# Loading K and V tiles through GpSimd's descriptor queue instead of SyncE's, in a decode kernel that streams 549 MB

## The chip, the cores and the metric

The kernel runs on one core of one Trainium2 chip. The metric is device time in microseconds (us). The kernel before took 1284.43 us as the median of 3 runs (1284.39 to 1284.6). Runs of one kernel agree within about 0.15%.

The names are those of the profile. PE is TensorE (matmuls), DVE is VectorE, ACT is ScalarE, POOL is GpSimd, SP is SyncE; SPq, POOLq and ACTq are loads that SyncE, GpSimd and ScalarE issue. A load goes from the large memory (HBM; the kernel before's page counts 549.03 MB read from it) to the core's own memory (SBUF) and is carried out by 16 DMA engines, as packets (12,975 of them on that page). The profile calls the queue of GpSimd's loads software_dynamic (q0) and those of SyncE and ScalarE hardware_dynamic (q1 and q10); "software queue" and "hardware queue" below mean these. A semaphore is a counter on which an engine can wait, here for a load to land (in the kernel before PE waits 3.2 us for wq) or for another engine's work (SyncE waits 18.0 us for PE's q projection).

## The reference

One decode step: an attention block over a long KV cache, mixed by a scalar gate with a gated MLP.

```
q      = x @ wq                                  # x: 1x448, wq: 448 x (16 heads x 256)
scores = (q . k_cache) / 16                      # 8 KV heads x 65536 keys x 256, bf16
a      = softmax(scores) @ v_cache  -> @ wo      # two query heads share a KV head
b      = ((gate * (gate > 0)) * up) @ W_down     # gate = x @ W_gate, up = x @ W_up, F = 1792
out    = g * a + (1 - g) * b                     # g = sigmoid(sum(x * gate_w))
```

K and V are 268 MB each and every byte is used once; everything else together is about 12 MB.

## The kernel before

K and V are cut into 32 tiles each, 128 partitions x 64 KB (8.4 MB) to a tile. Three such tiles fill the ring in SBUF. A tile of K is transposed in place on DVE and multiplied with q on PE (called QK); a tile of V is multiplied with the probabilities. "Gate/up" are W_gate and W_up together, four loads. The weights share a ring buffer: `wq`, then gate/up and `W_down`, live in buffer 2 before it becomes the home of K tile 2. Below, K0, K1, ... are tiles of K, V0, V1, ... tiles of V.

```python
# the order of the loads; each buffer is handed on round robin
order = [("wq", 0, 8.7), ("k", 0, TILE), ("gu", 0, 7.7), ("wd", 0, 3.8)]
for n in range(1, NT):
    order.append(("k", n, TILE))
    if n >= NTH - 1:
        order.append(("v", n - (NTH - 1), TILE))
# ... the last V tile in pieces, and wo ...

slot, held, freed = {}, {2: ["gu", "dn"]}, {}    # buffer 2 is free once gate/up and W_down were used on PE
r = 0
for kind, i, _ in order:
    if kind in ("k", "v") or (kind, i) in (("wo", 0), ("vp", 0)):
        slot[kind, i], freed[kind, i] = r, held.get(r, [])
        held[r] = [(kind, i)]
        r = (r + 1) % NRING
```

So K0 and K1 wait for nothing (buffers 0 and 1 start empty), K2 waits for `gu` and `dn` (the matmuls of gate/up and of W_down), and each later load waits for the matmuls that read its buffer last. Each engine runs its own list in order, and a wait holds up everything behind it in that list. In the kernel before SyncE waits 18.0 us for q in front of W_down, and K1, which itself waits for nothing, is issued behind W_down at 22.69 us. The lines of the program:

```python
# wq: two loads (rows of 24 KB, rows of 4 KB); q needs both
l_["wq"]  = dma("sp", t, "wq", ...)
l_["wqh"] = dma("sp", t + 0.01, "wqh", ...)
# W_down: goes where wq was, so it waits for the q projection
a3 = dma("sp", t, "wd", lambda e: e.dma_start(wd_sb, B_W_down...), [l_["q"]])
# a K tile
kd = dma("sp", t, "r%d" % sl, lambda e, n=n, sl=sl: e.dma_start(ring[sl][:], k_src(n)), free(("k", n)))
```

## Time and profile before

| | before |
|---|---|
| time, median | 1284.43 us |
| span of the profiled run | 1283.3 us |
| bytes loaded, mean rate | 549 MB, 428 GB/s |
| busy: DVE, PE, ACT, GpSimd | 49%, 33%, 5%, 0% |

Two parts of the kernel before's profile page: the share of DMA in 40 equal slices of the span (32 us each; tenths busy, and GB/s), and the queues (packets, MB, share of 16 engines' span).

```profile
DMA  9999999999999999999999999999999999999997
GB/s 398 431 436 432 432 437 432 432 434 432 436 427 436 434 434 429 432 436 434 429 432 437 434 434 432 436 427 432 435 438 425 432 440 434 430 427 440 431 408 313
...
q1 hardware_dynamic: 12930, 549.03, 99.2%
```

The stretches of the kernel before (us from the start; busy time and instruction counts of each engine; the last three columns are the granted PE clock, the DMA share and GB/s):

```profile
core 0: us, PE busy (x) PEld busy (x) DVE busy (x) ACT busy (x) POOL busy (x), PEclk, DMA share, GB/s
0.00:32.00 32.00, 11.17 (x72) 8.37 (x72) 8.31 (x35) 1.86 (x3) 4.09 (x21) 0.89 0.95 398
32.00:64.00 32.00, 19.98 (x232) 15.70 (x232) 18.64 (x12) 1.40 (x2) 0.00 (x0) 0.61 1.02 431
64.00:96.00 32.00, 10.56 (x96) 2.88 (x96) 30.22 (x15) 1.40 (x2) 0.00 (x0) 0.55 1.01 437
...
128.00:1240.00 1112.00, 356.50 (x3905) 126.46 (x3905) 550.24 (x343) 53.72 (x104) 0.00 (x0) 0.62 1.00 433
```

The DMA engines are never idle between the first microseconds and the tail: their share is 0.95 in the first 32 us and 1.00 to 1.02 in the stretches from there to 1240 us, and 433 GB/s were held for 1112 us. The kernel is bound by bytes over rate (549 MB at 433 GB/s make 1268 of the 1283.3 us); in this kernel a microsecond without transfers anywhere is a microsecond lost.

How long loads take, in the kernel before (what is loaded, who issues it, how many, KB, median us from issue to landing):

```profile
ring<-in_A_wq_dram SPq DMA_DIRECT2D x1, 512.0 KB, 11.0
ring<-in_A_k_cache_dram SPq DMA_DIRECT2D x32, 51.8
ring<-in_A_v_cache_dram SPq DMA_DIRECT2D x31, 36.7
...
ring<-in_B_W_up_dram SPq DMA_DIRECT2D x1, 224.0 KB, 35.4
```

A tile needs 19.4 us of all engines (8.39 MB at 433 GB/s). Landing 36.7 and 51.8 us after issue means that loads queue: when a tile is issued, most of another tile or more is still ahead of it. By estimate, 17 us of other transfers (36.7 less 19.4) or more are in front of a tile when it is issued, against 0.33 us for an issue on SyncE, so this queue can hide what an issue costs.

SyncE's timeline (start, duration, what, how many; the last line merges K1, K2 and K3):

```profile
22.32 0.33 SPq L441 DMA_DIRECT2D ring<-in_B_W_down_dram  x1
22.69 37.56 SPq L452 DMA_DIRECT2D ring<-in_A_k_cache_dram  x3
```

K1 was issued at 22.69 us, directly after W_down. The chain of work that ended last, of the same kernel (start, duration, what), at the place where K2 is released:

```profile
52.92 5.17 PE ST L347 x54
58.09 1.34 PE A_ps L358 x27
59.44 0.33 SPq L452
59.81 43.62 DMA ring<-in_A_k_cache_dram
```

PE finishes QK of K0 (L347), then the W_down product (L358), and at 59.44 us K2 is issued. K2's first packet starts at 60.9 us, and the last packet of K1 ends at 63.2 us in the packet records: K2 arrives at the engines just in time. The slack is small: where the engines are idle (experiment 2), the first packet follows SyncE's issue of K2 by 0.96 us, so K2 was ready at about 60.4 us here, by estimate 0.5 us before the first engine came free and 2.8 us before the last.

### The profile page before, as it was taken

To read this page: it belongs to the slowest core of one execution; us is meant where nothing else is said; L and a number is where in the kernel's file an instruction comes from. 1 tells how busy PE (TensorE), PEld (TensorE's weight loads), DVE (VectorE), ACT (ScalarE), POOL (GpSimd) and SP (SyncE) were. 2 spreads that over 40 slices of the span, in tenths; PEclk is the share of its full clock that TensorE was granted. 3 is DMA by queue.
4 is the path that set the end of the run, shared out by engine and by line. 5 is a ranking of instruction groups with operands and counts; after the bars stand their busy time and mean duration, and the time that the engine had idled before them with its cause. 6 is when DMAs were issued, how large, how long until landed. Compare 5 with 4: busy or idle time off the path is not lost.

```text
span 1283.3 us, 9919 instructions
## 1 busy us (share of the span) xinstructions
PE 427.0 (33%) x4600; PEld 162.9 (13%) x4600; DVE 633.6 (49%) x421; ACT 61.5 (5%) x116; POOL 4.1 (0%) x21
## 2 busy tenths in 40 slices
PE   3633332334123432224331243321433323233235
PEld 2401110111001210001110111100111101011111
DVE  2597633465533655434555444555434555335600
ACT  0000000000000000000000000000000000000000
POOL 1000000000000000000000000000000000000000
PEclk8656666656666565667665666655666656666567
DMA  9999999999999999999999999999999999999997
GB/s 398 431 436 432 432 437 432 432 434 432 436 427 436 434 434 429 432 436 434 429 432 437 434 434 432 436 427 432 435 438 425 432 440 434 430 427 440 431 408 313
DMA packets 12975, 549.67 MB, mean 428 GB/s; under 512 B 1283, under 2 KB 3590, under 8 KB 3974
## 3 DMA queue, kind: packets, MB, share of 16 engines
q1 hardware_dynamic: 12930, 549.03, 99.2%
q8 instruction: 36, 0.59, 0.2%
q14 instruction: 5, 0.04, 0.0%
q10 hardware_dynamic: 4, 0.00, 0.0%
HBM read 549.03 MB, written 0.00 MB: 428 GB/s over the span
## 4 chain that ended last, share of the span: by engine, by line
DVE 34%; DMA 32%; another core or an unknown queue 16%; PE 15%; SPq 1%; ACT 1%; issue 1%
DVE ring L335 30%; DMA ring<-in_A_k_cache_dram 27%; PE ST L347 7%; PE O L378 6%; DMA ring<-in_B_W_up_dram 3%; DMA ring<-in_A_wo_dram 2%; DVE P_sb L480 1%; SPq L521 1%; DVE nmb L458 1%; PE PT L485 1%; PE M_ps L429 1%; PE M_ps L432 0%; ACT ptp L494 0%; DVE o_sb L389 0%
## 5 line engine op out<-in xcount | busy, mean ns | idle before, releaser
L335 DVE STREAM_TRANSPOSE ring<-ring 128x2048 uint32<-128x2048 uint32 x256 | 565.4, 2275 | 410.0 <-DMA ring<-in_A_k_cache_dram 410.0
L347 PE MATMUL ST<-ring,xm 128*16 128x512 bf16 x2048 | 224.2, 612 | 755.2 <-DVE ring L335 755.2
L347 PEld LDWEIGHTS ST<-ring,xm 128*16 128x16 bf16 x2048 | 61.9, 120 | 903.0 <-DVE ring L335 794.6
L378 PE MATMUL O<-ring,ptp 128*4 128x512 bf16 x2048 | 149.0, 453 | 34.3 <-DMA ring<-in_A_v_cache_dram 30.3
L460 ACT ACTIVATE P_sb<-ST,nmb 128x512 bf16<-128x512 f32 x32 | 45.3, 1414 | 1112.7 <-DVE nmb L458 1112.7
L458 DVE TENSOR_REDUCE nmb<-ST 128x1 f32<-128x512 f32 x32 | 22.0, 689 | 110.7 <-PE ST L347 110.7
L378 PEld LDWEIGHTS O<-ring,ptp 128*4 128x4 bf16 x2048 | 54.5, 99 | 128.5 <-issue 58.3
L389 DVE CAST o_sb<-O 128x512 bf16<-128x512 f32 x8 | 5.5, 692 | 80.5 <-PE O L378 80.5
L480 DVE TENSOR_TENSOR P_sb<-P_sb,hs 128x1024 bf16<-128x1024 bf16 x16 | 18.9, 1222 | 8.7 <-ACT hs L474 8.7
L485 PE MATMUL PT<-identb,P_sb 128*128 128x128 bf16 x128 | 16.6, 310 | 15.5 <-DVE P_sb L480 14.7
L429 PE MATMUL M_ps<-xT,ring 128*128 128x1 bf16 x84 | 9.4, 205 | 16.3 <-DMA ring<-in_B_W_up_dram 16.3
L485 PEld LDWEIGHTS PT<-identb,P_sb 128*128 128x128 bf16 x128 | 12.3, 140 | 18.3 <-DVE P_sb L480 18.3
L494 ACT COPY ptp<-PT 128x256 bf16<-128x256 bf16 x32 | 10.3, 375 | 23.0 <-PE PT L485 23.0
L307 PE MATMUL M_ps<-ring,P_sb 128*128 128x256 bf16 x64 | 10.1, 335 | 3.2 <-DMA ring<-in_A_wq_dram 3.2
L429 PEld LDWEIGHTS M_ps<-xT,ring 128*128 128x128 bf16 x84 | 7.2, 151 | 16.9 <-issue 16.5
L460 ACT ACTIVATION_READ_ACCUMULATOR P_sb<-ST,nmb 128x1 f32 x32 | 8.5, 267 | 0.0
L307 PEld LDWEIGHTS M_ps<-ring,P_sb 128*128 128x128 bf16 x64 | 7.6, 120 | 5.5 <-issue 3.3
L432 PE MATMUL M_ps<-xT,ring 128*64 128x1 bf16 x56 | 7.8, 276 | 0.0
L412 DVE STREAM_TRANSPOSE ptp<-P_sb 128x128 uint32<-128x128 uint32 x1 | 0.3, 313 | 13.5 <-ACT P_sb L411 13.5
L470 PE MATMUL M_ps<-identf,hs 128*2 128x128 f32 x8 | 2.6, 321 | 10.0 <-DVE hs L468 10.0
L432 PEld LDWEIGHTS M_ps<-xT,ring 128*64 128x64 bf16 x56 | 5.4, 191 | 0.4
L358 PE MATMUL A_ps<-ring,attnT 128*1 128x224 bf16 x64 | 4.6, 305 | 2.5 <-DMA ring<-in_A_wo_dram 2.5
(72 smaller groups left out, 60.1 us busy)
## 6 DMA issues: line engine op xcount, KB each, us to landing
ring<-in_A_v_cache_dram SPq DMA_DIRECT2D x1, 4096.0 KB, 29.3
ring<-in_A_wq_dram SPq DMA_DIRECT2D x1, 3072.0 KB, 10.2
ring<-in_A_wo_dram SPq DMA_DIRECT2D x1, 2240.0 KB, 31.8
ring<-in_A_v_cache_dram SPq DMA_DIRECT2D x1, 2048.0 KB, 23.6
ring<-in_B_W_down_dram SPq DMA_DIRECT2D x1, 1568.0 KB, 20.6
ring<-in_B_W_gate_dram SPq DMA_DIRECT2D x1, 1344.0 KB, 32.6
ring<-in_B_W_up_dram SPq DMA_DIRECT2D x1, 1344.0 KB, 35.3
ring<-in_A_v_cache_dram SPq DMA_DIRECT2D x1, 1024.0 KB, 25.6
```

Source lines behind the costliest of these rows:

```text
L307: ins = e.matmul(QN_ps, xw3[:, k_, 31 - j:159 - j], rhs, start=(j == 0 and kt == 0), stop=(j == J - 1 and kt == R3))
L335: return lambda e: e.transpose(v, v)
L347: ins = e.matmul(bank[32 * w:32 * w + 16, :], xm[:, x0:x0 + 16], ktv[sl][:, u0:u0 + 16, c, :, r_], start=(b == 0 and c == 0 and r_ == 0), ...
L378: ins = e.matmul(OP[h % 2][32 * g:32 * g + 4, :], ptp[h % 2][:, col:col + 13:4], ring[sl][:, k * 512:(k + 1) * 512], start=(a == 0 and k < ...
L429: e.matmul(GU_ps[:, c:c + 1], wf3[which][:, kt * F + ft:(kt + 1) * F:FT], xT[:, kt:kt + 1], start=(kt == 0), stop=False, skip_group_check= ...
L432: ins = e.matmul(GU_ps[64 * half:64 * half + 64, c:c + 1], wfh[which][:, ft:F // 2:FT], xT[:, R3 + half:R3 + half + 1], start=False, stop= ...
L458: smax[n] = op("dv", tk + 22, lambda e, n=n, NM=NM, t_=t_: e.tensor_reduce(NM[:, t_:t_ + 1], ST[n % 2][:], AX.X, ALU.max, negate=True), [q ...
L460: aexp[n] = op("ac", tk + 23, lambda e, n=n, t_=t_, NM=NM, RS=RS: e.activation(P_sb[:, t_:2048:4], ST[n % 2][:], ACTF.Exp, bias=NM[:, t_:t ...
L480: rsc = op("dv", tt, lambda e, X=X, pb=pb: e.tensor_tensor(pb, pb, X[:, 12:16].unsqueeze(1).to_broadcast([128, 256, 4]), ALU.mult), [h7, a ...
L485: ins = e.transpose(PT[rd][:, s * 128:(s + 1) * 128], P_sb[:, (rd * 8 + s) * 128:(rd * 8 + s + 1) * 128], identb[:, :])
L494: ins = e.copy(dst, src)
L521: dep = dma("sp", t, "vp%d" % i, lambda e, sl=sl, n=n, lo=lo, hi=hi: e.dma_start(ring[sl][:, lo * 256:hi * 256], v_src(n)[:, lo * 256:hi * ...
```

## The change

The stated change is to load K and V tiles through GpSimd's descriptor queue instead of SyncE's. The queue's kind changes (software_dynamic in the profile, not hardware_dynamic), and so does which list a load stands in. K0 stays on SyncE with a semaphore of its own, because this program counts a semaphore's landings in the order of one engine's list.

```diff
-                kd = dma("sp", t, "r%d" % sl, lambda e, n=n, sl=sl: e.dma_start(ring[sl][:], k_src(n)), free(("k", n)))
+                kd = dma("sp" if n == 0 else "gp", t, "rk0" if n == 0 else "r%d" % sl, lambda e, n=n, sl=sl: e.dma_start(ring[sl][:], k_src(n)), free(("k", n)))
 ...
-                    dep = dma("sp", t, "r%d" % sl, lambda e, sl=sl, n=n: e.dma_start(ring[sl][:], v_src(n)), free(("v", n)))
+                    dep = dma("gp", t, "r%d" % sl, lambda e, sl=sl, n=n: e.dma_start(ring[sl][:], v_src(n)), free(("v", n)))
```

The order of instructions on PE, DVE and ACT is the same in both kernels. On GpSimd, 62 loads follow the 17 small setup instructions. On SyncE, the weights, K0, wo and the pieces of the last V tile remain.

## The prediction

> **What bounds the kernel now.** The page's queue part has queue 1 at 99.2% of 16 engines' span; the slices hold 425 to 440 GB/s nearly throughout, and the stage table gives a DMA share of 1.00 and 433 GB/s from 128 to 1240 us. DVE (49%) and PE (33%) have slack. The packet records show the tiles as 64 KB packets, median 2.42 us each. So time is bytes over rate, plus about 2 us of start and 5 of tail.[...]
>
> **What the change does.** 62 tile loads (K tiles 1 to 31, V tiles 0 to 30) move from SyncE's instruction stream to GpSimd's; bytes, buffers and the orders on PE, DVE and ACT stay. Weights, K tile 0 and the last V tile (in pieces) stay on SyncE.
>
> *Steady state.* Loads are issued when their buffer comes free: K tiles a median 51.8 us before landing, V tiles 36.7, against 19.4 us of transfer each. So most of a tile is queued ahead[...].[...] Cost about 0, plus an unknown small rate difference.
>
> *Start: the real cost.* Before, K1 sits behind the W_down load in SyncE's stream, which waits for the q projection: issued at 22.7 us. After, K1 waits for nothing and leaves GpSimd at about 7 us (its last setup instruction ends at 6.0).[...] With 64 KB packets on one side and the remaining 24 KB and 4 KB wq packets on the other, nearly all of K1's 8 packets per engine pass before wq is complete: wq lands at about 30 us instead of 12, q ends at 40 (22.3), K0 lands at 49 (31.5), gate/up at 57 (39.1), W_down at 61. Then PE needs gate/up (13.5 us), QK of K0 (5.2) and W_down (1.3) before K2 may overwrite the weights' buffer: issued at about 77 us instead of 59.4. All issued so far has landed by about 61, and K3 stands behind K2. So the DMA engines idle for about 17 us that a DMA-bound kernel never gets back. Before, K2 was issued about 3 us before K1 ended.
>
> *End.* wo's 1792-byte packets now alternate with V29's and V30's 64 KB ones: V30 lands about 1 us later. Cost 0 to 2 us.
>
> **Prediction.** 1284.4 + 17 (start) + about 2 (end, issue latency, rate) = **1303 us**, range 1287 to 1316. Faster by over 2%: 0.01; within: 0.74; slower: 0.25.
>
> **What would show it.** The stage table at 60 to 80 us nearly without DMA; wq and gate/up landing about 18 us later (L307's wait); K2's issue near 77 us; 433 GB/s after 128 us; short issues on GpSimd.
>
> **What would make it wrong.** If software descriptors are cut into small packets (4 KB), SyncE's loads win the round robin and the gap shrinks to about 4 us: time near 1290.[...]

The sum is 1284.4 + 17 (the start) + about 2 (the end, the latency of issues, the rate), which is 1303 us. At the marks, passages are cut that rested on no trace or run of this case but stood behind some of its terms and odds: a bound on the rate (behind the 0.01 for "faster by over 2%"), what hides the cost of an issue (behind "Cost about 0" and the latency of issues), how the engines serve two queues (behind the landings at the start, and so behind the 17 us), and two of the dangers (behind the 0.25 for "slower"). "The round robin" in the danger that remains is engines taking turns between two queues by packet; the trace of the changed kernel and experiment 8 show it, below.

## More of the kernel before

In SyncE's list K1 stands behind W_down, which waits for q. That order, not a dependency, keeps K1 away from the loads of the start.

## The result, and the profile after

| | before | after |
|---|---|---|
| time, median | 1284.51 us (4 runs: the 3 above and one more) | 1303.18 us (4 runs, 1302.92 to 1303.93) |
| span of the profiled run | 1283.3 us | 1301.1 us |
| ratio | | 1.0144, 95% interval 1.013 to 1.0159 |

Ratios here and below are the mean time of one kernel's runs over that of the other's runs of the same rounds, so not quite the ratio of the medians quoted. The 18.7 us are far outside the noise.

The same two parts of the changed kernel's page:

```profile
DMA  9859999999999999999999999999999999999997
GB/s 403 374 226 450 422 438 428 440 426 440 428 432 439 424 436 436 432 440 425 438 424 438 430 438 430 436 433 428 438 430 436 428 438 428 436 430 440 427 416 325
...
q0 software_dynamic: 8928, 520.10, 92.5%
q1 hardware_dynamic: 4002, 28.94, 5.4%
```

92.5% of the engines' time now belongs to the software queue. There is one hole, in the second and third slices (374 and 226 GB/s). The stretches of the changed kernel:

```profile
0.00:32.00 32.00, 1.12 (x9) 0.95 (x10) 5.94 (x24) 1.49 (x2) 4.78 (x22) 1.00 0.98 410
32.00:64.00 32.00, 15.12 (x120) 12.37 (x118) 14.93 (x16) 0.37 (x1) 0.00 (x0) 0.69 0.89 380
64.00:96.00 32.00, 18.56 (x215) 12.11 (x219) 23.30 (x14) 1.40 (x2) 1.06 (x2) 0.61 0.53 222
...
128.00:1240.00 1112.00, 352.52 (x3856) 124.34 (x3860) 563.66 (x353) 55.50 (x108) 30.08 (x57) 0.61 1.00 433
```

The last line is the important negative finding: over 1112 us the software queue moved data at 433 GB/s, the rate of the hardware queue to three digits. The packet records say the same: 7936 packets of 64 KB at a mean of 2425.2 ns, against 8064 at 2424.8 ns before. The loss lies in the stretches from 32 to 64 us (share 0.89 instead of 1.02) and from 64 to 96 us (0.53 instead of 1.01). In the packet records no packet of a kernel's load runs from 61.9 to 80.4 us: a gap of 18.5 us, against a difference of 18.7 us in time.

Loads of the changed kernel:

```profile
ring<-in_A_wq_dram SPq DMA_DIRECT2D x1, 512.0 KB, 30.5
ring<-in_A_k_cache_dram POOLq DMA_DIRECT2D x31, 51.9
ring<-in_A_v_cache_dram POOLq DMA_DIRECT2D x31, 36.7
...
ring<-in_B_W_up_dram SPq DMA_DIRECT2D x1, 224.0 KB, 54.8
...
ring<-in_A_k_cache_dram SPq DMA_DIRECT2D x1, 49.3
```

In the steady state K and V tiles take as long from issue to landing as before (51.9 and 36.7 us). The rest of the start is late by one tile: the small part of wq (512 KB, the rows of 4 KB) lands 30.5 us after issue instead of 11.0, the last part of gate/up 54.8 instead of 35.4 (19.4 us later, which is one tile's transfer).

GpSimd's timeline (start, duration, what, how many, and in brackets its idle time before and who ended it; the second line merges K2 and K3):

```profile
5.95 0.74 POOL L452 DMA_DIRECT2D ring<-in_A_k_cache_dram  x1
79.16 1.06 POOL L452 DMA_DIRECT2D ring<-in_A_k_cache_dram  x2 [72.46 <-PE A_ps L358]
```

K1 leaves at 5.95 us instead of 22.69, before the data that precedes it in the order of use. Then GpSimd waits 72 us for PE, and K2 goes out at 79.16 instead of 59.44. The chain that ended last, at the same place as before:

```profile
72.39 5.11 PE ST L347 x52
77.50 1.36 PE A_ps L358 x28
78.86 0.30 issue
79.16 0.53 POOL ring L452
79.69 42.09 DMA ring<-in_A_k_cache_dram
```

PE's work in front of K2 is as long as before (5.1 and 1.4 us); it is done 19.4 us later.

How K1 gets ahead can be counted in the packet records. Between 10 and 31 us, 120 packets of K1 (64 KB, 2.42 us each) and 121 packets of wq's small part (4 KB, 0.16 us each) started, and 17 packets of K0 on engines that were through with wq: about one for one. The records don't name the engine, but joined by their times into 16 sequences they alternate: while K1 is under way, the next packet is of the other queue in 190 of 215 cases (where two engines change at once, the joining can mix them up). So in this trace the engines took turns between the two queues by packet, and 125 of K1's 128 packets had started when wq's last one ended, at 31.2 us. In bytes, 64 KB against 4 KB is a split of 16 to 1 in favour of the queue with the larger packets.

### The profile page after: what moved, and what is told of

Read it like the earlier page. It is cut to its first block, busy times and chain, and to the rows that moved or that the text cites. A ratio compares the mean times of both kernels' runs of the same rounds, so it can differ in the third digit from the quotient of the medians. Undisturbed runs are those within 1.5% of the kernel's fastest.

```text
span 1301.1 us, 9919 instructions
## 1 busy us (share of the span) xinstructions
PE 424.5 (33%) x4600; PEld 161.7 (12%) x4600; DVE 633.5 (49%) x421; ACT 61.6 (5%) x116; POOL 37.0 (3%) x83
## 3 DMA queue, kind: packets, MB, share of 16 engines
q0 software_dynamic: 8928, 520.10, 92.5%
## 4 chain that ended last, share of the span: by engine, by line
DVE 33%; DMA 31%; another core or an unknown queue 17%; PE 16%; SPq 1%; ACT 1%; issue 1%; POOL 0%
DVE ring L335 30%; DMA ring<-in_A_k_cache_dram 27%; PE ST L347 6%; PE O L378 6%; DMA ring<-in_A_wq_dram 2%; DMA ring<-in_A_wo_dram 2%; DVE P_sb L480 1%; SPq L521 1%; DVE nmb L458 1%; PE M_ps L307 1%; PE PT L485 1%; PE M_ps L429 1%; PE M_ps L432 0%; ACT ptp L494 0%
## 5 line engine op out<-in xcount | busy, mean ns | idle before, releaser
L378 PE MATMUL O<-ring,ptp 128*4 128x512 bf16 x2048 | 146.2, 447 | 34.6 <-DMA ring<-in_A_v_cache_dram 30.6
L378 PEld LDWEIGHTS O<-ring,ptp 128*4 128x4 bf16 x2048 | 53.7, 97 | 127.1 <-issue 54.8
L517 POOL DMA_DIRECT2D ring<-in_A_v_cache_dram x31 | 16.4, 528 | 945.4 <-PE ST L347 941.7
L452 POOL DMA_DIRECT2D ring<-in_A_k_cache_dram x31 | 16.6, 535 | 248.6 <-PE O L378 151.4
L307 PE MATMUL M_ps<-ring,P_sb 128*128 128x256 bf16 x64 | 10.0, 335 | 22.3 <-DMA ring<-in_A_wq_dram 22.3
L429 PE MATMUL M_ps<-xT,ring 128*128 128x1 bf16 x84 | 9.5, 205 | 16.3 <-DMA ring<-in_B_W_up_dram 16.3
## 6 DMA issues: line engine op xcount, KB each, us to landing
ring<-in_A_v_cache_dram SPq DMA_DIRECT2D x1, 4096.0 KB, 30.5
```

The costliest lines, as they stand in the source:

```text
L307: ins = e.matmul(QN_ps, xw3[:, k_, 31 - j:159 - j], rhs, start=(j == 0 and kt == 0), stop=(j == J - 1 and kt == R3))
L378: ins = e.matmul(OP[h % 2][32 * g:32 * g + 4, :], ptp[h % 2][:, col:col + 13:4], ring[sl][:, k * 512:(k + 1) * 512], start=(a == 0 and k < ...
L429: e.matmul(GU_ps[:, c:c + 1], wf3[which][:, kt * F + ft:(kt + 1) * F:FT], xT[:, kt:kt + 1], start=(kt == 0), stop=False, skip_group_check= ...
L452: kd = dma("sp" if n == 0 else "gp", t, "rk0" if n == 0 else "r%d" % sl, lambda e, n=n, sl=sl: e.dma_start(ring[sl][:], k_src(n)), free((" ...
L517: dep = dma("gp", t, "r%d" % sl, lambda e, sl=sl, n=n: e.dma_start(ring[sl][:], v_src(n)), free(("v", n)))
```

## The experiments

Each was correct; "before" was timed beside them on the same chip (1285.0 to 1285.2 us as the median of 7 runs in each of the three groups). Theory A is the prediction's: one gap in front of K2, because K1 pushes gate/up a tile later. Rival B blames the software path itself, for each load. Rival C blames the delay of wq and the q projection, the most visible symptom at the start.

### 1. K1 back on SyncE, the other 61 tile loads on GpSimd

```diff
-kd = dma("sp" if n == 0 else "gp", t, "rk0" if n == 0 else "r%d" % sl, ...)
+kd = dma("sp" if n <= 1 else "gp", t, "rk%d" % n if n <= 1 else "r%d" % sl, ...)
```

> Only K tile 1 goes back to SyncE's stream (behind the W_down load, issued near 22.7 us); the other 61 tile loads stay on GpSimd. Theory A (the loss is one gap of the DMA engines in front of K tile 2, because K1's early packets push gate/up a tile later; the software queue itself costs nothing): 1284.5 us, within 2; gate/up wait of PE ends near 39 us, K2 issued near 60 us, DMA share at or above 0.99 from 64 to 96 us. Rival B (each software-issued load costs some 0.3 us of latency or rate, 62 of them make 18.7 us): 1302 to 1303. Rival C (K1 delays wq and with it the q projection): as A, 1284.5.

Measured: 1285.17 us, ratio 0.9999 (0.9982 to 1.0015). Its stretch from 64 to 96 us:

```profile
64.00:96.00 32.00, 8.80 (x80) 2.46 (x84) 28.13 (x14) 1.40 (x2) 0.53 (x1) 0.55 0.99 426
```

Moving one load of 62 takes back the whole loss. B falls: 61 software-issued loads cost nothing that can be measured (the interval leaves room for about 2 us). The end is that of the changed kernel (wo still shares the engines with V29 and V30), so the end costs nothing beyond that either.

### 2. The kernel before, with only K1 on GpSimd

```diff
-kd = dma("sp", t, "r%d" % sl, ...)
+kd = dma("gp" if n == 1 else "sp", t, "rk%d" % n if n <= 1 else "r%d" % sl, ...)
```

> The kernel before with only K tile 1 moved to GpSimd (issued near 6 us); 61 tile loads stay on SyncE. Theory A: 1303 us, within 2, with DMA share about 0.53 from 64 to 96 us and gate/up complete near 57 us. Rival B (a cost for each software load): 1284.8, one load costs 0.3. Rival C: as A.

Measured: 1303.61 us, ratio 1.0142 (1.0127 to 1.0157). Its stretch from 64 to 96 us:

```profile
64.00:96.00 32.00, 18.91 (x211) 11.69 (x209) 22.87 (x14) 1.41 (x2) 0.00 (x0) 0.61 0.54 226
```

The gap runs from 61.8 to 80.3 us. One load alone makes the whole loss; with experiment 1 it is both necessary and sufficient.

### 3. The kernel before, with only K1 on ScalarE's hardware queue

```diff
-kd = dma("sp", t, "r%d" % sl, ...)
+kd = dma("ac" if n == 1 else "sp", -7 if n == 1 else t, "rk%d" % n if n <= 1 else "r%d" % sl, ...)
```

> The kernel before with only K tile 1 moved to ScalarE's hardware queue, issued near 1.5 us; no software descriptors at all. Theory A: the queue's kind doesn't matter, only that K1 runs beside the loads of the start: gap of 17 to 19 us in front of K2, 1302 to 1305 us. Rival B (software descriptors): 1284.5 us, within 1.

Measured: 1302.95 us, ratio 1.0137 (1.0121 to 1.0152), with no software queue in the kernel (its page lists none; K1's 8.39 MB are in q10, hardware_dynamic). Its stretch from 64 to 96 us:

```profile
64.00:96.00 32.00, 18.55 (x211) 11.97 (x211) 23.28 (x14) 1.40 (x2) 0.00 (x0) 0.61 0.54 230
```

So the kind of queue does not matter here (1302.95 us with K1 on ScalarE's hardware queue, 1303.61 with K1 on GpSimd's software queue). What matters is that K1 runs in a queue beside SyncE's, early.

### 4. The changed kernel, with K1 waiting for the q projection

```diff
-..., free(("k", n)))
+..., free(("k", n)) + ([l_["q"]] if n == 1 else []))
```

> The changed kernel, but K1's load on GpSimd waits until the q projection is done, so wq is undisturbed and q ends near 22.3 us as before. Theory A (what counts is when gate/up lands, and K1's 19.4 us of packets still pass before it): gate/up complete near 57 to 58 us, K2 issued near 78 us, gap of 15 to 18 us, 1300 to 1303 us. Rival C (the delay of wq and q is the cause): K2 issued near 60 us, 1285 us, within 2.

Measured: 1303.43 us, ratio 1.0143 (1.0128 to 1.0158). K1 was issued at 22.22 us, half a microsecond earlier than in the kernel before, wq was undisturbed, and nothing was gained. K1 and K2 in GpSimd's timeline, then a load's landing and a wait of PE, from this run's loads and waits:

```profile
22.22 0.74 POOL L452 DMA_DIRECT2D ring<-in_A_k_cache_dram  x1 [16.22 <-PE M_ps L307]
79.27 1.06 POOL L452 DMA_DIRECT2D ring<-in_A_k_cache_dram  x2 [56.30 <-PE A_ps L358]
```

```profile
ring<-in_B_W_up_dram SPq DMA_DIRECT2D x1, 224.0 KB, 54.8
```

```profile
PE M_ps L429 <- DMA ring<-in_B_W_up_dram: 36.1, 1, 36.1
```

PE's wait for wq is 3.3 us (3.2 before, 22.3 in the changed kernel), and its wait for gate/up is 36.1 us instead of 16.3. Gate/up lands exactly as late as in the changed kernel, because K1's packets still pass before it; K2 is issued at 79.27 us. C falls. Compare with the kernel before: same issue time of K1, but there it stood behind gate/up in one queue, here it ran beside it in another. The issue time is not what counts; the order at the engines is.

### 5. The changed kernel, with K1 waiting until gate/up has landed

```diff
+                l_["a1"] = a1                       # the four loads of gate/up
 ...
-..., free(("k", n)))
+..., free(("k", n)) + (l_["a1"] if n == 1 else []))
```

> The changed kernel, all 62 tile loads on GpSimd, but K1's load waits until the gate/up weights have landed (near 39 us; W_down's 3.8 us of transfer covers the wait and the issue). Theory A: no gap, K2 issued near 60 us, DMA share at or above 0.98 from 64 to 96 us, 1284.5 to 1286.5 us. If something else of the software queue costs time (rate, latency, the end beside wo), that remainder shows here above 1286.5.

Measured: 1286.16 us, ratio 1.0008 (0.9993 to 1.0023): no gap, as predicted, and not to be told from before. Its stretch from 64 to 96 us:

```profile
64.00:96.00 32.00, 7.37 (x72) 2.05 (x76) 27.62 (x14) 1.39 (x2) 0.53 (x1) 0.55 0.99 429
```

All 62 loads can go through GpSimd at no cost that these runs can tell from noise (the interval leaves room for 3 us), if K1 is ordered behind gate/up by a semaphore that does what the single list did.

### 6. The changed kernel, with gate/up loaded before K0

```diff
-order = [("wq", 0, 8.7), ("k", 0, TILE), ("gu", 0, 7.7), ("wd", 0, 3.8)]
+order = [("wq", 0, 8.7), ("gu", 0, 7.7), ("k", 0, TILE), ("wd", 0, 3.8)]
```

> The changed kernel, K1 still issued near 6 us, but SyncE loads gate/up before K tile 0, so that PE can do gate/up and W_down before QK of K0. Theory A: wq still lands near 31 us, q ends near 42, gate/up has landed near 38, W_down lands near 62, K2 issued near 63 to 64 us: a gap of 2 to 4 us, 1286 to 1289 us. If K1's early issue cost something other than the late K2, 1300 or more.

Measured: 1290.46 us, ratio 1.0044 (1.0027 to 1.006), outside the expected 1286 to 1289. The direction is right (13 us of the loss are back), the size is not: the gap is 5.0 us (63.1 to 68.05). K2 was issued at 66.80 us, not at 63 to 64. W_down landed at 63.56 us instead of 62, and from there to the issue 3.2 us passed where the expectation left 1 to 2. The timeline shows most of that second part:

```profile
63.70 2.77 PE L358 MATMUL A_ps<-ring,hT 128*1 128x224 bf16 x28 [8.21 <-DMA ring<-in_B_W_down_dram]
```

The W_down product now follows W_down's landing directly. It took 2.77 us after 8.2 us of idle PE, against 1.51 us in the kernel before's timeline, directly behind other matmuls. (Whether the idle time before it made the product slower was not tested.)

### 7. The changed kernel, with only half of K1 issued early

```diff
+if n == 1:
+    kd  = dma("gp", t, "rk1a", ... ring[sl][:, 0:16384] ..., free(("k", n)))
+    kd2 = dma("gp", t, "rk1b", ... ring[sl][:, 16384:32768] ..., l_["a1"])   # after gate/up
 ...   # the last four of K1's eight transposes wait for kd2
```

> The changed kernel, but only half of K1 (4 MB) is issued near 6 us; the other half waits until gate/up has landed. Theory A: gate/up lands half a tile later (9.7 us, near 49 us), the gap is about half a tile less about 1 us of slack: 8 to 9.5 us, 1292 to 1295 us. A cost of any early concurrency that doesn't scale with its bytes (q late, one blocked queue): 1300 or more.

Measured: 1293.82 us, ratio 1.007 (1.0055 to 1.0085), with a gap of 8.85 us. The last part of gate/up:

```profile
ring<-in_B_W_up_dram SPq DMA_DIRECT2D x1, 224.0 KB, 45.2
```

That is 9.8 us later than before, half a tile. Half the bytes in front of gate/up make about half of the loss (8.8 of 18.7 us). The packets are halved too (128 of 32 KB), so their number in front of gate/up is that of the changed kernel: it is their bytes that count.

### 8. The changed kernel, with K1 as 16 loads of 4 KB rows

```diff
+for c in range(16 if n == 1 else 0):
+    kd = dma("gp", t, "rk1", ... ring[sl][:, c * 2048:(c + 1) * 2048] ..., free(("k", n)))
```

> The changed kernel, but K1 is loaded by 16 loads of 128 rows of 4 KB, all issued from GpSimd from about 6 us, instead of one of 128 rows of 64 KB: the same bytes, as early. Theory A with round robin by packet: each of SyncE's packets (4, 64, 10.7, 1.8 KB) now lets only one 4 KB packet of 0.16 us pass. From 7.5 us to the end of gate/up there are about 51 of SyncE's packets per engine, so gate/up lands about 8 us later than before (46 us), W_q's small half near 14 us, the gap is about 7 us, 1290 to 1293 us. If the engines share time or bytes evenly between the queues: gate/up again lands near 57 us, gap of 18 us, 1302 to 1304 us. If K1 only gets what SyncE leaves: no gap, 1285.

Measured: 1292.37 us, ratio 1.0054 (1.0037 to 1.0071), with a gap of 6.2 us (63.7 to 69.95). Gate/up:

```profile
ring<-in_B_W_up_dram SPq DMA_DIRECT2D x1, 224.0 KB, 43.4
```

That is 8.0 us later than before. The bytes and the time of the first issue (5.94 us) are those of the changed kernel; the size of a packet differs, and more than half of the loss is gone. (The 16 issues take 8.55 us together, 0.53 us for each 512 KB; the engines need about 1.2 us for as much at 433 GB/s, so the issuing did not hold K1 back.) By estimate, gate/up's 8.0 us of delay are about 50 of K1's packets per engine at 0.16 us each, against about 50 of SyncE's per engine from 7.5 us to the end of gate/up (a sixteenth of those in the packet records of the kernel before and of the changed one). So the engines take turns by packets here, neither by bytes nor by time: gate/up landed at 47.3 us, not near 57.

### The series

| kernel | gate/up lands later by (us) | gap (us) | longer than before by (us, medians) |
|---|---|---|---|
| before | 0 | none | 0 |
| K1 early in 4 KB packets (8) | 8.0 | 6.2 | 7.2 |
| half of K1 early (7) | 9.8 | 8.85 | 8.8 |
| changed kernel | 19.4 | 18.5 | 18.7 |
| K1 waits for q (4) | 19.4 | 18.65 | 18.2 |

The gap is the delay of gate/up less 0.8 to 1.8 us, which fits the slack of the kernel before.

No experiment pointed to a version that beats both kernels. The kernel before has no gap between its start and its tail to take back, and the software queue gives the same rate.

## Why the prediction was right

- *The bound.* Right. The DMA share from 128 to 1240 us was 1.00 before and after, at 433 GB/s in both.
- *Steady state free.* Right. K and V tiles land as long after issue as before, packets take the same 2.42 us, and experiment 1 (61 loads through GpSimd) is at 0.9999. GpSimd needs 0.53 us for an issue in the steady state against 0.33 us on SyncE. In the one place where an issue is exposed, at the end of the gap, 1.54 us pass from PE's last matmul to K2's first packet with GpSimd, and 0.98 us with SyncE (experiment 2). Elsewhere, by the estimate above, the 17 us of transfers in front of a tile can hide these 0.6 us, and experiment 1 shows no loss (0.9999).
- *K1 passes in front.* Right, and shown by the packet records (190 changes of queue in 215) and by experiment 8 (gate/up 8.0 us late instead of 19.4). The wording "wq lands at about 30 us" holds for its small part alone (31.7 us); the large part landed at 13.4 us. For q both are needed, so nothing hung on it.
- *The gap in front of K2.* Right in place and cause, shown by experiments 1 to 4 and 7. Its size was 18.5 us where the prediction had 17: I let gate/up be delayed by 18 us, but the whole tile of 19.4 us passes. The moments of the start came 1 to 2 us later than listed (K2 at 79.2, not 77).
- *The rest.* The prediction had about 2 us for the end, the latency of issues and the rate; 0.2 us are left for it (18.7 less 18.5). At the end wo's packets did alternate with those of V29 and V30: from 1248 to 1260 us, 84 packets of 1792 bytes and 77 of 64 KB started. Two small errors in the sum cancelled, so that 1303 against 1303.18 is closer than the terms were.
- *A part of the argument was not needed.* The prediction's chain went through wq and q. Experiment 4 shows that the delay of q is only a symptom: with q on time, gate/up and K2 were as late.
- *What was named as a danger.* No slower rate through the software queue appeared (433 GB/s in both kernels), and no gap after 128 us (DMA share 1.00): the 64 KB packets of the software queue lie between 2418 and 2433 ns at the 1st and 99th percentile, so no sixteenth of them, one engine's share, took longer by more than 1% throughout. Small software packets did shrink the gap in experiment 8, to 6.2 us, not to the estimate of 4.

## What to carry to other kernels

Moving a load to another engine's queue does more than change who issues it: it takes the load out of an order that may have been protecting something (here one load moved to a second queue cost 18.4 us, experiment 2). Before splitting one list of loads into two, ask which loads will run beside each other that used to run one after the other, which of them a wait depends on first, and whose packets are larger, since the engines took turns by packet here; then restore the order that matters with a semaphore (experiment 5). In a kernel bound by transfers, look for the one gap in the DMA share before blaming the rate: 18.7 us out of 1300 came from a single load at the start.
